# Channel attention and a gated layer, fp32 by split products: sums of squares by accumulating DMAs, high parts by ScalarE, and seven products for every pair of two more batches

## The chip, the cores and the metric

One core of a Trainium2 chip runs the whole program. The metric is the device time of one execution in microseconds. TensorE is called PE here (PEld is its weight load), VectorE DVE, ScalarE ACT, GpSimd POOL and SyncE SP.

## The reference

Four batches of q, k and v, each 6080 x 256, all float32; w_in is 256 x 2048 and w_out 2048 x 256, handed in as float64 words.

```python
qn = q / (norm(q, axis=1) + 1e-6)            # over the 6080 tokens
kn = k / (norm(k, axis=1) + 1e-6)
a  = softmax(kn.T @ qn / tau)                # 256 x 256 in each batch
x  = v @ a                                   # 24320 tokens x 256 in all
h  = x @ w_in                                # 24320 x 2048
g  = h / (1 + exp(-1.702 * h))
out = g @ w_out                              # 24320 x 256
```

## The kernel before

**Arithmetic.** A float32 product is made from parts: a high part (the value cast to fp32r) and a low part (what is left), and three matmuls, high by high, high by low and low by high (`three`, L780 in the traces). A high part is made by ACT (`cast`, L285) or, for q and k of batches 2 and 3, by a casting DMA from POOL's queue (`load_cast`, L282); a low part is a subtraction on DVE (`low`, L308). Other additions on DVE are `tt` (L293) and `minus` (L299).

**The main loop.** `a` and `w_in` are folded together for each batch, so the main loop makes `v @ (a @ w_in)`, the gate, and the product with `w_out`. A batch is cut into 6 chunks of tokens, five of 1024 and one of 960, and the 2048 hidden columns into 8 pairs of blocks. There are 4 x 6 x 8 = 192 pairs, in the order batch, chunk, pair. A pair is a product of 2 x 2 blocks, made in a Strassen-Winograd form with seven products. `front` makes the seven products before the gate into the banks X, Y and Z, with copies on ACT (ps_Y<-ps_X and others) between them, and the gate on ACT into `ga`. `back` makes the product with `w_out`, in one of two forms:

- with seven products (`is_s`): sums of blocks on DVE into `gp` (p13 of two blocks, p2, p4), their high and low parts in `gr` and `gj`, and three blocks of `ga` split into `gi`. Five products follow at once, two (`k6`, `k5`, from `gr`) at the end of the group;
- with eight: no sums, two blocks in `gi` and two in `gj`, eight products.

Pairs stand in groups, given by `groups_of`: `TWO = ((3, 1), (3, 1))` is two groups of three seven-product pairs and one eight-product pair; `THREE = ((3, 0), (3, 0), (2, 0))` has seven-product pairs alone. One bank, K, is shared within a group and is evacuated at its end three times (a, b, c), and once more (d) where the group has an eight-product pair: in the first group by ACT copies, later by additions on DVE. `groups_of` gives batch 0 (after its first chunk, which has eight products throughout) to batch 2 `TWO`, and batch 3 `THREE`.

**Preparation.** Beside the main loop of one batch the next ones are prepared. `Attention.unit` takes two tiles of 128 tokens of q and k at a time, 25 units a batch: raw tiles are loaded by SP into two buffers in turn (`ra0`, `ra1`); the scores k.T @ q go to PE (ps_s); ACT squares the raw tiles in place, and the squares are added into `acc` for the norms. For batches 2 and 3 the scores use parts: `hl` is one buffer with high and low. Batches 0 and 1 use the raw float32 values (`direct`). Batch 2's units are placed beside pairs 19 to 60, batch 3's beside 74 to 118; three pieces of softmax (`finish`) and eight `weights` follow each.

**The order.** `Plan` holds every operation with its engine, cost, lag, dependences, buffers and a due time. It places them by a list schedule forwards and backwards and emits each engine's instructions, the DMA issues of SP and POOL among them, in that fixed order. Weights come from HBM for each pair: `w` (two buffers), `wo` (three) and, for seven-product pairs, `wb`.

Of the kernel before, what the change touches and what calls it, by code (L numbers as in the profile page):

```python
# [11 lines left out]
F32 = mybir.dt.float32  # L12
# [3 lines left out]
ALU = mybir.AluOpType  # L16
# [4 lines left out]
P = 128  # L21
# [4 lines left out]
HW = CH // 2  # L26
# [162 lines left out]
FIRST = ((0, 4), (0, 4))  # L189


def groups_of(b, c):

    if b == c == 0:
        return FIRST
    return (TWO, TWO, TWO, THREE)[b]


NV = 8
# [8 lines left out]
def channel_attention_then_glu(  # L208
# [10 lines left out]
    nc = tc.nc  # L219
# [3 lines left out]
    NPAIR = DFF // (2 * P)  # L223
# [57 lines left out]
    def load_cast(dst, src, kb, deps=(), uses=(), due=0.0):  # L281
        return g.add("POOL", 800, lambda: nc.gpsimd.dma_start(dst(), src()), deps, uses, due, lag=8000)  # L282
# [12 lines left out]
    def minus(dst, a, b, n, deps, uses, due):  # L295

        return g.add(
            "DVE", dve(n),
            lambda: nc.vector.scalar_tensor_tensor(  # L299
                dst(), in0=a(), scalar=-1.0, in1=b(), op0=ALU.mult, op1=ALU.subtract,  # L300
            ),
            deps, uses, due,
        )

    def low(dst, src, hi, n, deps, uses, due):
# [132 lines left out]
    class Attention:  # L438
# [39 lines left out]
        def unit(self, u, due, after=()):  # L478
            t0, nt, pp = self.units[u]
            if t0 not in self.raw:  # L480
                t = sbuf(f"ra{u % 2}", [P, 2, UT, C], F32, "raw")
                view = (lambda i: t()[:, i, :nt, :]) if pp == P else (lambda i: t()[:pp, i, 0, :])
                ns = [
                    load(
                        lambda i=i: view(i), lambda i=i: self.rows(i, t0, nt, pp), 128 * nt, after, [t], due - 10, 7000,
                    )
                    for i in range(2)
                ]
                for o in range(nt):
                    self.raw[t0 + o] = (t, o, ns)  # L490
            buf, o, _ = self.raw[t0]
            ready = [n for j in range(nt) for n in self.raw[t0 + j][2]]
            w = 2 * nt * C
            src = lambda: buf()[:pp, :, o : o + nt, :]
            acc = self.acc
            if self.direct:
                ok, uses = ready, [buf]
            else:
                hl = sbuf("hl", [P, 2, UT, 2, C], F32R, "hl")
                hs = [  # L500
                    load_cast(
                        lambda i=i: hl()[:, i, :nt, 0, :] if pp == P else hl()[:pp, i, 0, 0, :],
                        lambda i=i: self.rows(i, t0, nt, pp), 128 * nt, after, [hl], due - 9,
                    )
                    for i in range(2)
                ]
                l = low(
                    lambda: hl()[:pp, :, :nt, 1, :], src, lambda: hl()[:pp, :, :nt, 0, :], w,
                    hs + ready, [buf, hl], due,
                )  # L510
                ok, uses = [l], [hl]
            S = self.S if self.direct else bank("Z", "s")
            news = []
            for j in range(nt):
                first = j == 0 and (u == 0 or not self.direct)

                def fn(j=j, first=first):
                    for i in range(NC2):
                        ci = slice(i * P, (i + 1) * P)
                        out = S()[:, i * C : (i + 1) * C]  # L520
                        begin = first and i == 0
                        if self.direct:
                            nc.tensor.matmul(  # L523
                                out, lhsT=buf()[:pp, 1, o + j, ci], rhs=buf()[:pp, 0, o + j, :],
                                start=begin, stop=True, skip_group_check=True,
                            )
                            continue
                        for m, (l, r) in enumerate(((0, 0), (0, 1), (1, 0))):
                            nc.tensor.matmul(  # L529
                                out, lhsT=hl()[:pp, 1, j, l, ci], rhs=hl()[:pp, 0, j, r, :],  # L530
                                start=begin and m == 0, stop=True, skip_group_check=True,
                            )

                n = g.add(
                    "PE", 864 if self.direct else 720, fn, ok + [self.first] + news[:1], [*uses, S], due + 2 + 0.1 * j,
                )
                if first and self.direct:
                    self.first = n
                news.append(n)
            if u == 0:  # L540
                self.acc_n = [g.add(
                    "ACT", act(w), lambda: nc.scalar.activation(acc(), src(), AF.Square), ok, [buf, acc], due + 0.5,
                )]
            else:

                sq = buf if self.b else sbuf(f"w{u % 2}", [P, 2, UT, C], F32, "sq")
                sqv = (lambda: src()) if self.b else (lambda: sq()[:pp, :, :nt, :])
                if self.b == 1:
                    ok = news
                s = g.add(  # L550
                    "ACT", act(w),
                    lambda: nc.scalar.activation(sqv(), src(), AF.Square), ok, [buf, sq], due + 1,
                )
                a = lambda: acc()[:pp, :, :nt, :]
                self.acc_n = [tt(
                    a, a, sqv, ALU.add, w, [s, *self.acc_n], [sq, acc], due + 1.5,
                )]
            if self.direct:
                self.last += news
            else:  # L560
                total = self.S
                self.last = [
                    g.add("DVE", dve(HW), lambda: nc.vector.tensor_copy(total(), S()), news, [S, total], due + 2.5)
                    if u == 0 else
                    tt(
                        lambda: total(), lambda: S(), lambda: total(), ALU.add, HW, news + self.last, [S, total],
                        due + 2.5,
                    )
                ]
# [150 lines left out]
    def values(b, c, due, after=(), eng="DVE"):  # L720
        o, w = chunks[c]
        hw = w // 2
        raw = sbuf("vr", [P, NC2, CH], F32, "v_raw")
        src = vT[b, :, o : o + w].rearrange("(c p) n -> p c n", p=P)
        r = load(lambda: raw()[:, :, :w], lambda: src, 1024, after, [raw], due - 40)
        blk = lambda j, n: (lambda: raw()[:, j, n * hw : (n + 1) * hw])
        B11, B12, B21, B22 = blk(0, 0), blk(0, 1), blk(1, 0), blk(1, 1)
        done = {}

        def split(m, x, deps, at, uses):  # L730
            t = sbuf(f"v{vslot[0] % NV}", [P, 2, HW], F32R, "v")
            vslot[0] += 1
            h = cast(lambda: t()[:, 0, :hw], x, hw, deps, [*uses, t], at)
            l = low(lambda: t()[:, 1, :hw], x, lambda: t()[:, 0, :hw], hw, [h], [*uses, t], at + 0.3)
            done[m] = (t, l)
            return l


        vt = sbuf("vt", [P, HW], F32, "v_t")
        P1 = lambda: vt()[:, :hw]  # L740
        p1 = tt(P1, B11, B12, ALU.add, hw, [r], [raw, vt], due - 20, eng)
        p3 = tt(B12, B12, B22, ALU.add, hw, [p1], [raw], due - 16, eng)
        split(M5, P1, [p1], due, [vt])
        s11 = split(M1, B11, [r, p1], due + 0.7, [raw])
        s21 = split(M2, B21, [r], due + 2, [raw])
        p2 = tt(B11, P1, B22, ALU.add, hw, [p1, s11], [raw, vt], due + 2.2, eng)
        split(M6, B11, [p2], due + 2.5, [raw])
        split(M7, B12, [p3], due + 4, [raw])
        split(M3, B22, [r, p3], due + 4.5, [raw])
        p4 = tt(B21, B21, B11, ALU.add, hw, [p2, s21], [raw], due + 3, eng)  # L750
        split(M4, B21, [p4], due + 6, [raw])
        return done
# [79 lines left out]
    def back(ck, u, fr, wo, wb, t):  # L832
# [87 lines left out]
        def evac(name, deps, at):  # L920
            prev = ck.tot.get(name)
            if prev is None:
                s = sbuf("k" + name, [P, HW], F32, "k" + name)
                n = cast(lambda: s()[:, :hw], lambda: K[0]()[:, :hw], hw, deps, [K[0], s], at, psum=True)
            else:
                s = prev[0]
                n = tt(
                    lambda: s()[:, :hw], lambda: K[0]()[:, :hw], lambda: s()[:, :hw], ALU.add, hw,
                    [*deps, prev[1]], [K[0], s], at,
                )  # L930
            ck.tot[name] = (s, n)
            return n
# [226 lines left out]
```

## Time and profile before

| | us |
|---|---|
| median of 3 runs | 2116.87 |
| lowest, highest | 2116.82, 2120.28 |
| the profiled execution, its own time | 2116.12 |
| its span in the trace | 2114.4 |
| PE, DVE, ACT busy | 2082.2, 1918.6, 1620.3 |

The span runs from the first instruction to the last. A busy time is the union of an engine's instructions; PE's matmuls overlap in its pipe, so a PE that is busy all the time need not issue at its full rate, and the distance between starts says more.

### The profile page before, as it was taken

The page shows a single profiled execution, that of the slowest core. Times are in us where ns is not written, and L with a number is a line of the kernel's source. Part 1 is how long each engine was busy: PE and PEld are TensorE (multiplying, and loading weights), DVE is VectorE, ACT ScalarE, POOL GpSimd, SP SyncE. Part 2 cuts the span into 40 slices and gives each one's busy share as a digit, 9 for nine tenths or more (in the row PEclk, how much of TensorE's full clock was granted, in tenths as well). Part 3 has the DMA queues.
Part 4 walks back from the last instruction along what each step waited for, and adds up shares of the span by engine and source line. Part 5 has one row for each costly group of instructions (what it writes and reads, how often), then busy time and mean ns, then how long its engine had stood idle before and what let it go on. Part 6 is the DMA issues. An engine that isn't in the chain of part 4 may idle for free.

```text
span 2114.4 us, 27101 instructions
## 1 busy us (share of the span) xinstructions
PE 2082.2 (98%) x9658; PEld 1737.6 (82%) x9658; DVE 1918.6 (91%) x2395; ACT 1620.3 (77%) x2361; POOL 76.7 (4%) x110
## 2 busy tenths in 40 slices
PE   9799999999999999999999999999999999999998
PEld 8688787888888888888888888888888888888887
DVE  8898898989999989889989898898988999999997
ACT  6677886877777877878767777778787778778875
POOL 0000001000000000000000000000000000000000
PEclk9899999999999999999999999999999999999999
DMA  9997787777777567877776776668756656665663
GB/s 352 333 338 263 264 291 264 255 236 250 253 254 265 192 235 260 296 263 255 244 258 214 264 266 216 212 217 290 281 189 219 226 208 212 232 231 186 245 213 130
DMA packets 210135, 521.90 MB, mean 247 GB/s; under 512 B 16464, under 2 KB 88144, under 8 KB 208976
## 3 DMA queue, kind: packets, MB, share of 16 engines
q1 hardware_dynamic: 184080, 495.25, 65.9%
q0 software_dynamic: 25920, 24.91, 5.1%
q8 instruction: 77, 1.26, 0.2%
q14 instruction: 58, 0.48, 0.1%
HBM read 453.25 MB, written 66.85 MB: 246 GB/s over the span
## 4 chain that ended last, share of the span: by engine, by line
PE 80%; DVE 9%; DMA 6%; ACT 3%; issue 1%; SPq 1%; POOL 0%; DVEq 0%; ACTq 0%
PE ps_o L780 23%; PE ps_X L780 16%; PE ps_k L780 14%; PE ps_Y L780 11%; PE ps_Z L780 10%; PE ps_s L529 3%; PE ps_w L696 2%; DMA hl<-in_k 2%; DVE gp L293 1%; PE ps_s L523 1%; DVE gi L308 1%; DMA out_T<-oc 1%; DVE ga L293 1%; DMA v_raw<-in_vT 1%; DVE acc L293 1%
## 5 line engine op out<-in xcount | busy, mean ns | idle before, releaser
L780 PE MATMUL ps_X<-v,w 128*128 128x512 f32 (+1 forms) x1728 | 485.1, 389 | 0.8 <-ACT ps_Z L285 0.7
L780 PEld LDWEIGHTS ps_X<-v,w 128*128 128x128 f32 x1728 | 321.2, 188 | 68.7 <-ACT ps_Z L285 3.1
L780 PE MATMUL ps_o<-gi,wo 128*128 128x512 f32 (+1 forms) x1404 | 375.7, 388 | 1.3 <-DVE gi L308 1.3
L806 ACT ACTIVATE ga<-ga 128x512 f32<-128x512 f32 (+1 forms) x384 | 238.4, 627 | 163.0 <-DVE ga L293 161.5
L308 DVE TENSOR_TENSOR gi<-ga,gi 128x1536 fp32r<-128x1536 f32 (+2 forms) x192 | 311.1, 1621 | 27.4 <-ACT gi L285 26.6
L780 PE MATMUL ps_Y<-v,w 128*128 128x512 f32 (+1 forms) x1152 | 325.5, 391 | 3.9 <-ACT ps_Y L285 2.5
L780 PE MATMUL ps_Z<-v,w 128*128 128x512 f32 (+1 forms) x1152 | 323.7, 389 | 1.0 <-ACT ps_Z L285 0.5
L780 PE MATMUL ps_o<-gj,wo 128*128 128x512 f32 (+1 forms) x1152 | 310.6, 389 | 1.1 <-DVE gj L308 0.7
L780 PEld LDWEIGHTS ps_o<-gi,wo 128*128 128x128 f32 x1404 | 262.7, 188 | 54.5 <-DVE gi L308 1.6
L285 ACT CAST gi<-ga 128x1536 fp32r<-128x1536 f32 (+2 forms) x192 | 264.3, 1376 | 7.7 <-PE ps_k L780 3.0
L780 PEld LDWEIGHTS ps_Z<-v,w 128*128 128x128 f32 x1152 | 215.0, 188 | 47.9 <-ACT ps_Z L285 2.5
L780 PEld LDWEIGHTS ps_o<-gj,wo 128*128 128x128 f32 x1152 | 215.2, 188 | 46.3 <-DVE gj L308 1.7
L780 PEld LDWEIGHTS ps_Y<-v,w 128*128 128x128 f32 x1152 | 212.2, 188 | 49.5 <-ACT ps_Y L285 5.9
L780 PE MATMUL ps_k<-gr,wb 128*128 128x512 f32 (+1 forms) x900 | 239.6, 388 | 0.0
L308 DVE TENSOR_TENSOR gr<-gp,gr 128x1024 fp32r<-128x1024 f32 (+1 forms) x150 | 181.0, 1207 | 23.2 <-ACT gr L285 23.2
L293 DVE TENSOR_TENSOR gp<-ga 128x1024 f32<-128x1024 f32 (+1 forms) x150 | 181.4, 1209 | 21.1 <-ACT ga L806 18.1
L780 PEld LDWEIGHTS ps_k<-gr,wb 128*128 128x128 f32 x900 | 168.3, 188 | 34.0 <-DVE kb L293 0.3
L308 DVE TENSOR_TENSOR gj<-gp,gj 128x1024 fp32r<-128x1024 f32 (+1 forms) x150 | 181.0, 1206 | 9.9 <-ACT gj L285 9.8
L285 ACT CAST gr<-gp 128x1024 fp32r<-128x1024 f32 (+1 forms) x150 | 156.2, 1042 | 43.9 <-DVE gp L293 33.4
L285 ACT CAST gj<-gp 128x1024 fp32r<-128x1024 f32 (+1 forms) x150 | 156.2, 1041 | 8.4 <-DVE gp L293 7.4
L293 DVE TENSOR_TENSOR ga<-ps_Y,m 128x512 f32<-128x512 f32 (+1 forms) x192 | 130.4, 679 | 25.9 <-PE ps_Y L780 25.4
L285 ACT COPY ps_Y<-ps_X 128x512 f32<-128x512 f32 (+1 forms) x192 | 110.7, 577 | 52.4 <-PE ps_X L780 51.2
(120 smaller groups left out, 2783.9 us busy)
## 6 DMA issues: line engine op xcount, KB each, us to landing
w<-w_d SPq DMA_DIRECT2D x184, 896.0 KB, 5.3
wo<-wout_d SPq DMA_DIRECT2D x150, 640.0 KB, 5.5
wb<-wout_d SPq DMA_DIRECT2D x150, 256.0 KB, 4.7
wo<-wout_d SPq DMA_DIRECT2D x42, 512.0 KB, 5.8
w_d<-wst SPq DMA_DIRECT2D x24, 896.0 KB, 6.1
v_raw<-in_vT SPq DMA_DIRECT2D x20, 1024.0 KB, 8.3
out_T<-oc SPq DMA_DIRECT2D x80, 256.0 KB, 5.1
wi<-win_d SPq DMA_DIRECT2D x32, 512.0 KB, 5.2
```

The lines of the kernel that those rows point to most:

```text
L285: return g.add("ACT", act(n, psum), lambda: nc.scalar.copy(dst(), src()), deps, uses, due)
L293: return g.add("DVE", dve(n), lambda: nc.vector.tensor_tensor(dst(), a(), b(), op=op), deps, uses, due)
L308: lambda: nc.vector.tensor_tensor(dst(), src(), hi().bitcast(F32), op=ALU.subtract),
L523: nc.tensor.matmul(out, lhsT=buf()[:pp, 1, o + j, ci], rhs=buf()[:pp, 0, o + j, :], start=begin, stop=True, skip_group_check=True,)
L529: nc.tensor.matmul(out, lhsT=hl()[:pp, 1, j, l, ci], rhs=hl()[:pp, 0, j, r, :], start=begin and m == 0, stop=True, skip_group_check=True,)
L696: nc.tensor.matmul(pb()[:, i * 2 * P : (i + 1) * 2 * P], lhsT=at.aT()[:, l, j, ci], rhs=wi()[:, m, j, :], start=i == 0 and n == 0, stop=Tr ...
L780: nc.tensor.matmul(dst, lhsT=l(a), rhs=r(b), start=begin and n == 0, stop=True, skip_group_check=True,)
L806: lambda: nc.scalar.activation(dst(), src(), AF.Gelu_apprx_sigmoid, scale=sign), deps, uses, at,
```

## The change

Three things change. The squares of q and k of batches 2 and 3 are still made by ACT in place, but are added into `acc` by a DMA from POOL's queue that accumulates (SBUF to SBUF, `add_dma`), not by DVE; the planner is told of a lag of 9 us. The high parts of q and k of these batches are one ACT cast from the raw tile, in place of two casting DMAs. And batches 1 and 2 get `THREE` in place of `TWO`. The switches VSUM and KSUM are off, so their branches (in `values` and in `evac`) emit nothing.

```diff
+VSUM = lambda b, c: False
+QSUM = lambda b: b >= 2
+HIACT = True
+KSUM = 0
+ALAG = 9000
...
-    return (TWO, TWO, TWO, THREE)[b]
+    return (TWO, THREE, THREE, THREE)[b]
...
+    def add_dma(dst, more, deps, uses, due):
+
+        return g.add(
+            "POOL", 1200, lambda: nc.gpsimd.dma_start(dst(), more(), accum_op=ALU.add), deps, uses, due, lag=ALAG,
+        )
...
                 hs = [
+                    cast(lambda: hl()[:pp, :, :nt, 0, :], src, w, ready, [buf, hl], due - 1)
+                ] if HIACT else [
                     load_cast(
...
-                self.acc_n = [tt(
-                    a, a, sqv, ALU.add, w, [s, *self.acc_n], [sq, acc], due + 1.5,
-                )]
+                if QSUM(self.b):
+                    self.acc_n = [add_dma(a, sqv, [s, *self.acc_n], [sq, acc], due + 1.5)]
+                else:
+                    self.acc_n = [tt(
+                        a, a, sqv, ALU.add, w, [s, *self.acc_n], [sq, acc], due + 1.5,
+                    )]
```

## Rows read from the trace of the kernel before

**Rows 1.** The page: busy times, granted clock in 40 slices, the casting DMAs' queue.
```profile
PE 2082.2 (98%) x9658; PEld 1737.6 (82%) x9658; DVE 1918.6 (91%) x2395; ACT 1620.3 (77%) x2361; POOL 76.7 (4%) x110
...
PEclk9899999999999999999999999999999999999999
...
q0 software_dynamic: 25920, 24.91, 5.1%
```

**Rows 2.** Timeline of PE alone, in batch 0: start, us, what, [idle before].
```profile
327.63 0.84 PE L780 MATMUL ps_o<-gj,wo 128*128 128x512 f32 x3
328.31 0.84 PE L780 MATMUL ps_X<-v,w 128*128 128x512 f32 x3
...
331.03 0.84 PE L780 MATMUL ps_o<-gi,wo 128*128 128x512 f32 x3
332.69 0.36 PE L529 MATMUL ps_s<-hl 128*128 128x256 f32 x1 [0.81 <-DMA hl<-in_k]
333.91 1.57 PE L529 MATMUL ps_s<-hl 128*128 128x256 f32 x11 [0.87 <-DVE hl L308]
```

**Rows 3.** Busy times by stretch: batch 0 after chunk 0, batch 1, batch 2.
```profile
core 0: us, PE busy (x) PEld busy (x) DVE busy (x) ACT busy (x) POOL busy (x), PEclk, DMA share, GB/s
...
204.10:635.50 431.40, 426.67 (x2027) 356.55 (x2027) 390.43 (x480) 332.91 (x487) 28.36 (x39) 1.00 0.76 257
635.50:1143.60 508.10, 505.19 (x2390) 423.69 (x2389) 460.90 (x565) 394.19 (x580) 30.03 (x41) 1.00 0.74 251
1143.60:1637.40 493.80, 492.22 (x2286) 410.74 (x2285) 438.13 (x540) 384.26 (x567) 16.43 (x23) 1.00 0.68 238
```

**Rows 4.** The same in batch 3: chunk 1, chunk 4, chunks 1 to 4.
```profile
1718.70:1792.10 73.40, 73.40 (x324) 60.25 (x323) 71.28 (x84) 60.66 (x90) 0.00 (x0) 1.00 0.60 216
...
1949.00:2022.30 73.30, 73.23 (x321) 59.65 (x320) 70.27 (x83) 58.62 (x87) 0.00 (x0) 1.00 0.63 225
...
1718.70:2022.30 303.60, 303.40 (x1328) 247.71 (x1327) 292.90 (x341) 246.21 (x357) 0.00 (x0) 1.00 0.62 220
```

**Rows 5.** Timeline of DVE alone, in batch 0.
```profile
313.50 1.21 DVE L293 TENSOR_TENSOR gp<-ga 128x1024 f32<-128x1024 f32 x1
314.63 1.75 DVE L308 TENSOR_TENSOR gi<-ga,gi 128x1536 fp32r<-128x1536 f32 x1
316.30 0.68 DVE L299 SCALAR_TENSOR_TENSOR oc<-ps_o,kc 128x512 f32<-128x512 f32 x1
316.90 0.68 DVE L293 TENSOR_TENSOR kd<-ps_k,kd 128x512 f32<-128x512 f32 x1
```

**Rows 6.** The stretches of rows 3, DVE's instructions on the tile acc alone.
```profile
204.10:635.50 431.40, 20.73 (x17) 1.00 0.76 257
635.50:1143.60 508.10, 22.78 (x20) 1.00 0.74 251
1143.60:1637.40 493.80, 14.23 (x13) 1.00 0.68 238
```

**Rows 7.** Busy times in the stretch with batch 2's weights (columns as rows 3).
```profile
719.50:890.60 171.10, 169.31 (x801) 141.21 (x800) 152.15 (x207) 134.23 (x201) 3.12 (x3) 1.00 0.69 250
```

**Rows 8.** The tile hl: its casting DMAs (issue, count), and landings.
```profile
L282 POOL DMA_DIRECT2D hl<-in_k x50: 527/721/736, 320.5 to 1339.8; - x50
...
DMA to landing us min/median/max: 2.1/6.0/12.0
```

**Rows 9.** The tile raw in batches 0 to 2: additions of squares (first, last start), landings.
```profile
L293 DVE TENSOR_TENSOR acc<-acc,raw x48: 675/1218/1227, 347.0 to 1353.8; 128x1024 f32<-128x1024 f32 x44, 128x512 f32<-128x512 f32 x2, 64x512 f32<-64x512 f32 x2
...
DMA to landing us min/median/max: 2.6/5.8/8.8
```

**Rows 10.** ACT's groups in batches 1 and 2: count, busy, mean ns, idle before.
```profile
L285 ACT CAST gi<-ga 128x1536 fp32r<-128x1536 f32 x60 | 89.0, 1484 | 4.6 <-PE ps_k L780 2.4 <-PE ps_o L780 1.0
L285 ACT CAST gr<-gp 128x1024 fp32r<-128x1024 f32 x60 | 63.1, 1052 | 16.0 <-DVE gp L293 13.1 <-PE ps_k L780 2.7
```

**Rows 11.** The chain that ended last, in order of time: start, us, what.
```profile
320.52 9.52 DMA hl<-in_k
330.04 2.59 issue
...
349.51 8.72 DMA hl<-in_k
...
1173.45 8.57 DMA hl<-in_k
```

## What was predicted

> **What bounds the kernel now.** I read the page first: PE is busy 98% of the span and its granted clock, the PEclk line, is full but for the first slices [rows 1]. That matmul busy time counts a matmul's wait in the pipe too, so I went on to the pace: in a timeline of PE alone three matmuls of 512 columns start every 0.68 us, 0.2267 us each, and this hardly changes for whole stretches [rows 2]. Then the busy times by stretch [rows 3]: batch 0 after its first chunk, batch 1, batch 2. The reader is to see two things. PE is busy almost throughout, and DVE has 9.5%, 9.3% and 11.3% left. So PE sets the time, through the number of its matmuls, and DVE is the second engine close behind. Batch 3 shows what the seven-product form alone looks like, since it has it already: over four chunks without any preparation of scores or weights, PE issued 1328 matmuls in 303.6 us, 0.2286 us each, 0.8% over its pace, while DVE was busy 96.5%; in the first of these chunks DVE was busy 97.1% [rows 4]. That is the fullest DVE that the trace shows, and PE hardly suffered from it.
>
> **PE: the term that gains.** A pair without the seven products makes 8 products of 3 matmuls behind the gate (24), one with them 7 (21). Batches 1 and 2 have 6 chunks each with two such pairs: 24 pairs, 72 matmuls fewer. Sixty have 512 columns, 60 x 0.2267 = 13.6 us; the twelve of the two short chunks have 480, by share 0.2126 us each, 2.6 us. Together 16.2 us. PE sets the pace there, so all of it counts unless another engine takes over. Batches 1 and 2 took 508.1 + 493.8 = 1001.9 us; PE alone would make that 985.7.
>
> **DVE: the term that takes some back.** What one more DVE instruction costs is read from the distance between starts, as consecutive ones overlap by 0.08 us: 1.13 us for 1024 elements, 1.67 for 1536, 0.60 for 512 [rows 5]. Such a pair gains the two-block sum (1.13), two single sums (2 x 0.60), the low part of gr (1.13), and its gi is of three blocks instead of two (1.67 - 1.13 = 0.54); the low part of gj was there before, in another form. That is 4.0 us. A chunk also evacuates K nine times instead of eight, six of them by additions on DVE instead of four: 2 x 0.60. So 2 x 4.0 + 1.2 = 9.2 us a chunk, 8.7 at 480 columns, 10 x 9.2 + 2 x 8.7 = 109.4 us in all.
>
> Against it the additions of the squares go. In these two batches they are 19 and 12 (20 and 13 rows less the one addition of each softmax) [rows 6]: 22.78 + 14.23 less 2 x 0.68 and less an overlap of 0.086 each make 33.0 us. DVE was busy 460.90 + 438.13 = 899.0 us [rows 3]; it will be 899.0 + 109.4 - 33.0 = 975.4. In 985.7 us that is 99.0%, above anything that the trace shows. In the stretch with the weights of batch 2 it is worse: 152.15 us of 171.1 [rows 7] become 152.2 + 18.4 - 1.1 = 169.5, in 168.4 us of PE. There DVE must hold PE up.
>
> What two engines that are both nearly full lose to each other no row shows. Bounds: if DVE can be filled no further than the 97.1% of rows 4, the two batches take 975.4 / 0.971 = 1004.5 us, 2.6 more than now; if it can be filled wholly, 985.7, 16.2 less. At 97.1% PE lost almost nothing, so the limit lies above it; but as the weights' stretch does not fit, I take 98.0%, nearer the row: 995.3 us, 6.6 less than now.
>
> By a rule of the Trainium skill ("VectorE: DVE Perf Modes", section "The DRAIN you can't avoid") a DVE instruction waits until the pipe of the one before is empty, and chaining doesn't avoid it; the same section allows an earlier start where nothing holds the instruction. Taken strictly it would add the 0.086 us to each instruction and make this change a loss (the last rival below). The trace does not agree: the start at 314.63 us lies before the end of the instruction at 313.50, which took 1.21 [rows 5].
>
> **The squares by DMA.** Forty-eight additions leave DVE (17 of them in batch 0, where PE is the bound and their 19 us are worth nothing by themselves) and become DMAs from POOL's queue. POOL has nothing else to do then; its 100 casting DMAs go. The accumulate moves 512 KB and also reads its target. Nearest rows: the casting DMAs, 256 KB at most, land in 6.0 us in the median and 12.0 at most [rows 8], the raw loads of the same units in 2.6 to 8.8 us [rows 9]. I bound it by 2 and 18 us (one and a half times the longest), and take 9. What waits for it: the next accumulate, behind it in POOL's queue, and the raw buffer, which the load two units later needs. A unit comes every 17.0 us ((635.5 - 347.0) / 17) [rows 6, 9], so each of two buffers has 34 us; load, cast, low part and square take 5.8 + 1.05 + 1.13 + 1.06 = 9.0 us, which leaves 25 us with the waits in between. So no cost up to about 20 us. Beyond that the raw load blocks SP's queue, with the w, wo and wb loads behind it.
>
> **The high parts by ScalarE.** Fifty casts of 1024 elements at 1.05 us [rows 10] come onto ACT, 31 or so in these two batches (33 us). The 24 pairs add one cast of gr (1.05) and widen gi (1.48 - 1.05), 35 us, less 12 evacuations of 0.58. ACT goes from 394.19 + 384.26 = 778 to about 840 us in 990, 85% [rows 3]; in rows 4 it ran at 82.6% (60.66 of 73.40) without harm. Cost nothing, hidden beside PE; if that cover went, it would show as ps_Y and ps_Z evacuations late. In return the low part no longer waits for a casting DMA, whose landings are in the chain: the first of batch 0 took 9.52 us and 2.59 more until its waiter started [rows 11], and PE stood from 331.71 (331.03 and three starts of 0.2267) to 332.69, and again, after one matmul of 0.12, to 333.91 [rows 2]: 2.1 us. Of the three other long ones in the chain [rows 11] I count nothing, which leaves up to 2 us unclaimed. So 2.1 us less, between 0 and 4.
>
> The added wb loads (24 of 256 KB) and wider wo are 9 MB, less than the 24.91 MB of q and k that the casting queue read a second time [rows 1]; DMA share is 0.74 or below in both batches [rows 3]. Nothing. Head, batch 0's other chunks, batch 3 and the tail are as before: nothing, give or take a few us by which the replanned order shifts.
>
> **Sum.** 2116.1 us of the profiled execution (span 2114.4 and 1.7 around it) - 6.6 - 2.1 = 2107.4. The median of the runs shown, 2116.87, lies 0.8 higher, which makes 2108; with the bounds of DVE's limit leaning to the better side, as PE lost nothing at 97.1%, I give 2107.
>
> **Rivals.**
> PE keeps its pace in full, DVE follows at 99%: 2116.1 - 16.2 - 2.1 = 2098, up to 2 less if the small stalls shrink. For it: rows 4, where DVE is at 97.1% and PE undisturbed. Against: the weights' stretches, which don't fit.
> DVE takes back everything: at 97.1 to 97.4% the two batches come out at 1001.4 to 1004.5 us, total 2113 to 2117: no change. The point that decides is 975.4 / 1001.9 = 97.4%.
> Slower, one mechanism: DVE becomes the bound in batches 1 and 2 and needs more idle time than 2.6%. Place: the group ends and the weights' stretches, where a gi low part waits for its cast on ACT while nothing else is ready. At 95.9%, the share of the chunk at 1949.0 [rows 4], 975.4 / 0.959 = 1017.1 us, 15.2 more: 2129. Against it: in that chunk PE set the pace, so DVE's idle time there is what PE left.
> The accumulates are late: over 20 us each, the raw loads hold up SP's queue. At 25 us it is 5 us on some 48 units, of which I take half as hidden by w's second buffer: about 120 us slower, 2230. Against it: none of the casting DMAs took over 12.0 us [rows 8].
> DVE instructions that don't overlap: 565 + 540 [rows 3] + 120 - 31 = 1194 instructions of 0.086 us, up to 103 us: 1078 us for the two batches, 2192.
>
> **Chances.** The forecast (2102 to 2112) 0.47; PE in full 0.25; no change 0.15; DVE the bound 0.09; late accumulates 0.03; no overlap 0.01. What a measurement here tells from no change is about 0.2%, 4.2 us: faster is below 2112.6, and the first two cases make 0.72; same 0.16, with a little of the forecast's edge; slower 0.12. The range takes in the PE-bound case and the no-change case to a little way into the slower one: 2096 to 2122.
>
> **What would show it.** PE's matmuls should be 9586 (9658 - 72); DVE busy over batches 1 and 2 near 975 us and its idle time in them 1 to 3%; no low part of hl waiting for a DMA; 48 accumulates, landing under 20 us, with no SP wait on them of note. More PE waits on DVE (ga, gi, gp, gr) in batches 1 and 2 are expected, most of them about the weights. Wrong would be: the batches not shorter though DVE idles over 3%, which would mean latency along one chain, not load; a stretch in which w or wo arrive late behind a raw load; or batch 3 changed.

## The result, and the profile after

The changed kernel takes 2099.72 us in the median of 4 runs (2096.14 to 2101.60), the kernel before on the same chip 2118.57 us (2116.82 to 2121.57): ratio 0.9911, 95% interval 0.9899 to 0.9923, or 18.9 us. The forecast was 2107 (2096 to 2122). The profiled execution of the changed kernel took 2096.14 us, its fastest, and its span is 20.1 us shorter than that of before. The profiled execution of before lies 2.5 us under the median of its runs here, that of the change 3.6, so differences of spans lean some 1.2 us to the better side, and stretches of the change alone some 3 us.

From the page of the kernel after, the lines that answer to [rows 1]; instructions have other line numbers now (L780 became L815, L285 L292, L293 L300, L308 L321, L523 L538, L593 L611):

```profile
PE 2063.3 (99%) x9586; PEld 1723.9 (82%) x9586; DVE 1966.3 (94%) x2467; ACT 1691.6 (81%) x2423; POOL 49.7 (2%) x58
...
PEclk9999999999999999999999999999999999999999
...
q0 software_dynamic: 7168, 23.86, 6.4%
```

PE has the 72 matmuls less that were counted, at the same full granted clock. Busy times by stretch of the kernel after: up to the first pair of batch 1, batch 1, batch 2, both batches, the rest. And of the kernel before, the first stretch and both batches in one (columns as in [rows 3]):

```profile
0.00:625.90 625.90, 610.30 (x2902) 513.08 (x2903) 549.41 (x749) 488.38 (x695) 18.40 (x26) 0.99 0.84 281
625.90:1133.40 507.50, 502.91 (x2378) 421.36 (x2377) 492.24 (x609) 425.66 (x608) 17.38 (x19) 1.00 0.77 259
1133.40:1617.60 484.20, 482.25 (x2246) 403.44 (x2245) 473.38 (x587) 404.57 (x585) 13.89 (x13) 1.00 0.74 252
625.90:1617.60 991.70, 985.15 (x4622) 824.81 (x4621) 965.62 (x1195) 830.23 (x1191) 31.27 (x32) 1.00 0.75 256
1617.60:2094.30 476.70, 467.86 (x2066) 385.99 (x2064) 451.29 (x525) 372.95 (x540) 0.00 (x0) 1.00 0.60 211
```

```profile
0.00:635.50 635.50, 615.63 (x2916) 516.48 (x2917) 570.69 (x770) 470.53 (x676) 30.19 (x46) 0.99 0.81 279
635.50:1637.40 1001.90, 997.41 (x4674) 834.43 (x4673) 899.03 (x1104) 778.45 (x1146) 46.46 (x64) 1.00 0.71 244
```

The first stretch lost 9.6 us, both batches 10.2, the rest 0.3 (477.0 to 476.7). Work slips over the cuts: of the 72 matmuls 14 are missing in the first stretch, 52 in the two batches, 6 in the rest. The 14 are products of batch 0's own last chunk (480 columns) that stand behind the cut now; at 0.2126 us they are 3.0 us, so 6.6 us of the first stretch came from something else. The 52 are 11.8 us at 0.2267, of which 1.6 were lost. PE's waits in the two batches of the kernel after, all of them (us, times, longest):

```profile
PE ps_Z L815 <- DMA w<-w_d: 5.2, 5, 2.5
PE ps_t L683 <- ACT ga L841: 0.9, 1, 0.9
PE ps_k L815 <- DVE gi L321: 0.4, 1, 0.4
```

So its matmuls waited for late loads of w (0.5 us before) and hardly for DVE. DVE is at 97.0% in batch 1 and 97.8% in batch 2. A single chunk of batch 2 shows that it goes further:

```profile
1465.60:1545.10 79.50, 79.50 (x363) 66.15 (x362) 79.21 (x100) 66.15 (x98) 0.00 (x0) 1.00 0.72 256
```

DVE is busy 79.21 of 79.50 us there, 99.6%, while PE issues 363 matmuls in them, 0.2190 us each, no slower than in [rows 2] (there are short ones among them). The timeline of DVE alone, of the kernel after, in that chunk:

```profile
1489.42 1.76 DVE L321 TENSOR_TENSOR gi<-ga,gi 128x1536 fp32r<-128x1536 f32 x1
1491.09 1.23 DVE L300 TENSOR_TENSOR gp<-ga 128x1024 f32<-128x1024 f32 x1
1492.22 0.69 DVE L306 SCALAR_TENSOR_TENSOR oc<-ps_o,kc 128x512 f32<-128x512 f32 x1
1492.83 0.69 DVE L300 TENSOR_TENSOR ga<-ps_Y,m 128x512 f32<-128x512 f32 x1
```

Each instruction starts about 0.09 us before the one ahead of it ends, as in [rows 5]. The rule of the Trainium skill that the prediction weighed ("VectorE: DVE Perf Modes", section "The DRAIN you can't avoid"), taken strictly, would have given 2192 us; this trace does not bear that out.

The tiles hl and acc of the kernel after: the high parts' casts, the accumulates and their landings, and of SP's waits the one on an accumulate (us, times, longest):

```profile
L292 ACT CAST hl<-raw x50: 609/1051/1066, 325.9 to 1326.4; 128x1024 fp32r<-128x1024 f32 x46, 128x512 fp32r<-128x512 f32 x2, 64x512 fp32r<-64x512 f32 x2
```

```profile
L315 POOL DMA_DIRECT2D acc<-raw x48: 847/856/1214, 338.7 to 1336.1; - x48
...
DMA to landing us min/median/max: 3.6/6.1/11.2
```

```profile
SPq L285 <- DMA acc<-raw: 4.8, 3, 3.5
```

The accumulates land in 6.1 us in the median, and the raw loads wait 4.8 us for them in the whole run.

What changed in the first stretch is seen at its head, in the timeline of PE alone: first before, then after.

```profile
65.63 1.84 PE L593 MATMUL ps_n<-ones,acc 128*128 128x1 f32 x8 [8.80 <-DVE acc L293]
```

```profile
57.66 0.95 PE L611 MATMUL ps_n<-ones,acc 128*128 128x1 f32 x8
60.41 2.08 PE L538 MATMUL ps_s<-raw 128*128 128x256 f32 x4 [1.79 <-DMA raw<-in_k]
```

Before, PE stood 8.80 us until DVE had added the squares of batch 0. After, that wait is gone, though no operation of the head was changed. The wait also cost clock. From 59.6 to 73.3 us, before and after:

```profile
59.60:73.30 13.70, 7.67 (x22) 6.53 (x23) 12.45 (x27) 4.51 (x7) 1.13 (x1) 0.50 0.91 303
59.60:73.30 13.70, 12.89 (x54) 11.19 (x55) 11.77 (x27) 7.79 (x12) 1.03 (x1) 0.88 1.03 367
```

Before, the granted clock stood at 0.50, the lower level (1.2 GHz), after PE had come to a stand, and PE issued 22 matmuls; after, it was 0.88 in the mean, and PE issued 54. What changed in the head is the emitted order: DVE's first 149 instructions stand in another order than before (found from the two programs' lists of instructions).

### The profile page after: what moved, and what is told of

The parts are those of the page before. It is cut to its first block, busy times and chain, and to the rows that moved or that the text cites. A ratio compares the mean times of both kernels' runs of the same rounds, so it can differ in the third digit from the quotient of the medians.

```text
span 2094.3 us, 27083 instructions
## 1 busy us (share of the span) xinstructions
PE 2063.3 (99%) x9586; PEld 1723.9 (82%) x9586; DVE 1966.3 (94%) x2467; ACT 1691.6 (81%) x2423; POOL 49.7 (2%) x58
## 3 DMA queue, kind: packets, MB, share of 16 engines
q0 software_dynamic: 7168, 23.86, 6.4%
## 4 chain that ended last, share of the span: by engine, by line
PE 77%; DVE 10%; DMA 7%; issue 3%; ACT 3%; POOLq 0%; SPq 0%; POOL 0%; DVEq 0%; ACTq 0%
PE ps_o L815 21%; PE ps_X L815 15%; PE ps_k L815 15%; PE ps_Z L815 10%; PE ps_Y L815 10%; DMA w<-w_d 3%; PE ps_s L544 3%; DVE gp L300 2%; PE ps_w L714 2%; DVE gi L321 1%; DVE acc L300 1%; PE ps_s L538 1%; DVE ga L300 1%; DMA w_d<-wst 1%; DMA out_T<-oc 1%
## 5 line engine op out<-in xcount | busy, mean ns | idle before, releaser
L815 PE MATMUL ps_X<-v,w 128*128 128x512 f32 (+1 forms) x1728 | 484.6, 389 | 1.6 <-ACT ps_Z L292 1.5
L815 PEld LDWEIGHTS ps_X<-v,w 128*128 128x128 f32 x1728 | 321.8, 188 | 68.6 <-ACT ps_Z L292 3.8
L815 PE MATMUL ps_o<-gi,wo 128*128 128x512 f32 (+1 forms) x1260 | 340.2, 388 | 1.5 <-DVE gi L321 1.5
L321 DVE TENSOR_TENSOR gi<-ga,gi 128x1536 fp32r<-128x1536 f32 (+2 forms) x192 | 324.4, 1690 | 12.9 <-ACT gi L292 12.4
L815 PE MATMUL ps_Z<-v,w 128*128 128x512 f32 (+1 forms) x1152 | 324.3, 390 | 7.5 <-DMA w<-w_d 7.3
L815 PE MATMUL ps_Y<-v,w 128*128 128x512 f32 (+1 forms) x1152 | 324.2, 390 | 0.4 <-ACT ps_Y L292 0.4
L815 PE MATMUL ps_o<-gj,wo 128*128 128x512 f32 (+1 forms) x1152 | 315.1, 388 | 1.1 <-DVE gj L321 0.7
L292 ACT CAST gi<-ga 128x1536 fp32r<-128x1536 f32 (+2 forms) x192 | 274.7, 1431 | 5.2 <-PE ps_k L815 1.9
L815 PEld LDWEIGHTS ps_o<-gi,wo 128*128 128x128 f32 x1260 | 235.4, 188 | 49.4 <-DVE gi L321 2.7
L815 PE MATMUL ps_k<-gr,wb 128*128 128x512 f32 (+1 forms) x1044 | 273.6, 388 | 0.0
L815 PEld LDWEIGHTS ps_Z<-v,w 128*128 128x128 f32 x1152 | 214.9, 188 | 55.6 <-DVE gr L321 2.9
L815 PEld LDWEIGHTS ps_o<-gj,wo 128*128 128x128 f32 x1152 | 215.4, 188 | 45.4 <-DVE gj L321 1.1
L815 PEld LDWEIGHTS ps_Y<-v,w 128*128 128x128 f32 x1152 | 212.7, 188 | 44.4 <-ACT ps_Y L292 3.4
L300 DVE TENSOR_TENSOR gp<-ga 128x1024 f32<-128x1024 f32 (+1 forms) x174 | 210.9, 1212 | 19.6 <-ACT ga L841 16.5
L815 PEld LDWEIGHTS ps_k<-gr,wb 128*128 128x128 f32 x1044 | 195.0, 188 | 38.8 <-DVE kb L300 0.3
L321 DVE TENSOR_TENSOR gr<-gp,gr 128x1024 fp32r<-128x1024 f32 (+1 forms) x174 | 210.8, 1211 | 10.6 <-ACT gr L292 10.5
L321 DVE TENSOR_TENSOR gj<-gp,gj 128x1024 fp32r<-128x1024 f32 (+1 forms) x174 | 210.7, 1211 | 6.5 <-ACT gj L292 6.4
L292 ACT CAST gr<-gp 128x1024 fp32r<-128x1024 f32 (+1 forms) x174 | 181.1, 1041 | 36.7 <-DVE gp L300 27.9
L292 ACT CAST gj<-gp 128x1024 fp32r<-128x1024 f32 (+1 forms) x174 | 181.0, 1040 | 11.9 <-DVE gp L300 10.3
L292 ACT COPY ps_Y<-ps_X 128x512 f32<-128x512 f32 (+1 forms) x192 | 110.4, 575 | 56.0 <-PE ps_X L815 54.7
L815 PE MATMUL ps_k<-gi,wo 128*128 128x512 f32 (+1 forms) x522 | 146.5, 389 | 1.1 <-DMA wo<-wout_d 0.7
```

The source lines that it names most:

```text
L292: return g.add("ACT", act(n, psum), lambda: nc.scalar.copy(dst(), src()), deps, uses, due)
L300: return g.add("DVE", dve(n), lambda: nc.vector.tensor_tensor(dst(), a(), b(), op=op), deps, uses, due)
L321: lambda: nc.vector.tensor_tensor(dst(), src(), hi().bitcast(F32), op=ALU.subtract),
L815: nc.tensor.matmul(dst, lhsT=l(a), rhs=r(b), start=begin and n == 0, stop=True, skip_group_check=True,)
```

## The experiments

The theory after the result: PE's 72 matmuls are worth nearly their 16.2 us because DVE can be filled to about 99% and no further, and the rest comes from batch 0 and above all its head, where the list schedule came out better once the casting DMAs were gone. The rivals: the gain is the casting DMAs' own cost all along batches 0 to 2; the head's gain is the place of the sum of v, or any new order; the seven products would gain without DVE's relief.

All kernels are the changed one with switches set otherwise, except where it says "before". Times are medians; "less" is the difference to the median of the kernel before on the same chip, measured beside it.

| kernel | seven products | squares by DMA | high parts by ACT | us | less | ratio (95%) |
|---|---|---|---|---|---|---|
| the change | yes | yes | yes | 2099.72 | 18.9 | 0.9911 (0.9899-0.9923) |
| groups_only | yes | no | no | 2114.12 | 2.4 | 0.9982 (0.9970-0.9994) |
| no_groups | no | yes | yes | 2108.14 | 8.4 | 0.9957 (0.9942-0.9971) |
| high_only | no | no | yes | 2107.17 | 9.4 | 0.9955 (0.9940-0.9970) |
| groups_high | yes | no | yes | 2107.44 | 10.3 | 0.9958 (0.9943-0.9973) |
| groups_sums | yes | yes | no | 2122.80 | -5.0 | 1.0020 (1.0004-1.0037) |

**The parts alone and in pairs.** The seven products without the rest:

```diff
-QSUM = lambda b: b >= 2
-HIACT = True
+QSUM = lambda b: False
+HIACT = False
```

> Seven products for every pair in batches 1 and 2, but the squares' sums stay on DVE and the high parts on the casting DMAs. If DVE's relief is what lets PE's 16.2 us through: DVE would need 899.0 + 109.4 = 1008 us in these two batches, more than the 1001.9 us they took before, so they take 1010 to 1020 us, DVE idle under 1% in them, and the whole is 8 to 18 us slower than before (2126 to 2137). If the planner can hide DVE's work anyway: 2100 to 2104. In both the head stays at its 99.6 us before the first pair, since DVE's order there is that of before.

The rest without the seven products:

```diff
-    return (TWO, THREE, THREE, THREE)[b]
+    return (TWO, TWO, TWO, THREE)[b]
```

> The sums by DMA and the high parts by ScalarE, batches 1 and 2 as before (eight products in two pairs of a chunk). By the forecast: 2 us less, where a casting DMA came late in batch 0, and nothing for DVE's relief, 2115 to 2117. By the rival, that some 7 us of the gain come from the head, where this kernel has the order of the changed one (the sum of batch 0's squares ahead of v's blocks on DVE): 2107 to 2111, the head at 92 to 94 us instead of 99.6.

ScalarE's high parts alone (the edit of no_groups, and QSUM as in groups_only):

> High parts by ScalarE alone. The head has the order of the changed kernel here too. By the rival: head 92 to 94 us, 2107 to 2111. By the forecast: 2115 to 2117, the first late casting DMA of batch 0 (2.1 us) gone and nothing else.

The change without the accumulating DMAs (QSUM as in groups_only):

> Seven products and the high parts by ScalarE, the sums kept on DVE. By the theory that DVE can be filled to 98 or 99% and no further: batches 1 and 2 take 1001 to 1008 us, as with the groups alone (1004.6), DVE idle under 1.5% in them, and batch 1 starts 6 to 10 us earlier than before: 2106 to 2114. If the casting DMAs were what made the groups alone slow: 990 to 995 us, 2097 to 2103.

The seven products alone bring little (2.4 us), though they take the same 72 matmuls away. Both cases of their expectation missed: DVE's 1008 us came out as 992.66 busy, and the head did not stay as before. DVE stands in a third order there, PE's norms start without a wait, and the first stretch is 6.2 us shorter with 6 matmuls fewer:

```profile
55.07 0.95 PE L611 MATMUL ps_n<-ones,acc 128*128 128x1 f32 x8
```

```profile
0.00:629.30 629.30, 611.98 (x2910) 514.65 (x2911) 568.27 (x769) 470.67 (x676) 35.34 (x46) 0.99 0.81 282
```

So the 2.4 us are those of another order in batch 0; the two batches took 2.8 us more than before. Both batches in groups_only, then in groups_high:

```profile
629.30:1634.00 1004.70, 990.35 (x4615) 821.35 (x4614) 992.66 (x1224) 809.19 (x1159) 47.59 (x64) 1.00 0.73 253
```

```profile
627.30:1630.90 1003.60, 993.51 (x4628) 823.58 (x4628) 992.87 (x1226) 832.03 (x1192) 4.56 (x2) 1.00 0.67 239
```

Two kernels that differ in their high parts have the same DVE time and the same length: 98.8% and 98.9%. PE's share is 98.6% and 99.0% there, down from 99.6% before. This is DVE's limit. Beside ScalarE's high parts, the seven products alone add nothing measurable (2107.44 against 2107.17), the accumulates alone nothing (2108.14), both together some 8 us (2099.72). The accumulates are worth something only where the seven products fill DVE, as the prediction had it; ScalarE's high parts are worth 9.4 us by themselves, which it did not have; they lie in the first stretch (626.6 us in high_only), while its two batches took 1001.7 us, as before.

The change with the casting DMAs back (HIACT as in groups_only):

> Seven products and the sums by DMA, the casting DMAs kept. If DVE's relief is what batches 1 and 2 need and the high parts pay in the head and batch 0 alone: batches 1 and 2 take 988 to 995 us, as in the changed kernel (991.7), and batch 1 starts near 635 us as before, since DVE's order in the head is not that of the changed kernel: 2103 to 2110. If the high parts on ScalarE are also needed for the dense stretches: 995 to 1003 us there, 2108 to 2117.

This expectation missed: it is slower than before. In the stretch from 883 to 1300 us, batch 3's scores, its busy times, then those of the change:

```profile
883.00:1300.00 417.00, 404.58 (x1882) 335.97 (x1881) 393.80 (x464) 322.73 (x458) 50.17 (x64) 0.99 0.89 279
```

```profile
883.00:1300.00 417.00, 412.67 (x1950) 347.00 (x1949) 406.79 (x479) 353.32 (x498) 18.85 (x22) 1.00 0.80 261
```

The DMA engines are busy 89% of it, not 80%, and PE issues 68 matmuls fewer in the same time, 15.4 us at its pace. PE's waits there on w (us, times, longest) in groups_sums, two of its DMA issues with their KB and landing, and its timeline of POOL, where casting DMAs stand behind an accumulate that waits for ACT's squares:

```profile
PE ps_Z L815 <- DMA w<-w_d: 6.2, 5, 3.1
PE ps_X L815 <- DMA w<-w_d: 3.0, 1, 3.0
```

```profile
w<-w_d SPq DMA_DIRECT2D x39, 896.0 KB, 7.0
hl<-in_k POOLq DMA_DIRECT2D x22, 256.0 KB, 9.2
```

```profile
983.60 0.91 POOL L315 DMA_DIRECT2D acc<-raw  x1 [15.58 <-ACT raw L567]
984.19 1.06 POOL L289 DMA_DIRECT2D hl<-in_q  x1
984.89 1.09 POOL L289 DMA_DIRECT2D hl<-in_k  x1
```

The change, in that stretch:

```profile
PE ps_Z L815 <- DMA w<-w_d: 4.3, 3, 2.5
```

```profile
w<-w_d SPq DMA_DIRECT2D x40, 896.0 KB, 5.9
```

PE waited 4.9 us more for w than in the change, and 3.2 us for other things (1.1 of them for hl). Twice, about waits of 1.86 and 3.08 us, the granted clock stood at 0.50, the lower level, for 3.4 us; at half the pace the two cost at most 3.4 us together. That is 11.5 of the 15.4 us; the profiled execution (2118.1) is one of the faster ones. That the two sorts of DMA crowd each other, on POOL's queue and on the engines, is argued from these rows; how much each of these costs was not separated.

**DVE's limit by dose.** One of the additions of a pair is made twice, in 48 pairs of batches 1 and 2, 48 x 0.60 = 28.8 us.

```diff
+            if u % 2 == 0 and ck.b in (1, 2):
+                p2 = tt(lambda: gp()[:, 1, :hw], lambda: gp()[:, 0, :hw], blk(3), ALU.add, hw, [p2], [ga, gp], t + 9.5)
```

> The changed kernel with 48 additions of 512 elements made twice on DVE (p2, in every other pair of batches 1 and 2): 28.8 us more for DVE, which idles 26 us in them. If DVE has become the second bound there, 10 to 29 us slower than the changed kernel: 2110 to 2129. If PE alone sets the time: 2098 to 2102.

The same in a kernel with all three parts of the change undone:

> The same 48 additions made twice in the kernel before, where DVE idles 103 us in batches 1 and 2: 0 to 3 us slower, 2117 to 2120, by both theories. A longer time would mean that the added wait in the chain of the block sums costs, and not DVE's load.

On the change it gave 2113.66 us (ratio 0.9980, 0.9971 to 0.9991), 13.9 more than without it (14.8 with each taken against the kernel before beside it); on the kernel before 2116.27 (0.9996, 0.9987 to 1.0005), no difference. Both batches, in the change with the additions (its profiled execution is the slowest of ten):

```profile
630.80:1638.50 1007.70, 997.01 (x4634) 827.67 (x4633) 992.36 (x1245) 833.43 (x1196) 30.55 (x32) 1.00 0.76 253
```

Again 98.5%. Three programs stop at 98.5 to 98.9% over these batches, the change stays below at 965.62 / 991.70 = 97.4%, PE's pace setting the time.

**Where ScalarE's high parts gain.** With neither the seven products nor the accumulates, first with ACT's cast for one unit only, the first of batch 2, then for those of batch 3 only:

```diff
-                ] if HIACT else [
+                ] if self.b == 2 and u == 0 else [
```

> The kernel before, but one unit of 50, the first of batch 2, gets its high parts from ScalarE instead of two casting DMAs. DVE's first 149 instructions then stand in the order that they have in the changed kernel, and not in that of before. If the gain of the high parts (9 us) comes from how the head is ordered: batch 1 starts 6 to 9 us earlier (635.5 before) and the whole takes 2107 to 2111. If it is gathered at the late casting DMAs, unit by unit: 2.1 us for this unit's, 2114 to 2116.

```diff
-                ] if HIACT else [
+                ] if self.b == 3 else [
```

> The kernel before with the high parts of batch 3 alone by ScalarE, 25 units, not one of them in batch 0. DVE's first 149 instructions stand as in the kernel before. If the gain of the high parts is the head and the first unit: 0 to 2 us, 2115 to 2118, batch 1 starting within 3 us of 635.5. If each late casting DMA costs: 3 to 6 us faster.

The one unit of 50 gave 2108.03 us (0.9957, 0.9941 to 0.9974), 9.6 less than before, as much as all of them. The 25 units of batch 3 gave 2114.87 (0.9989, 0.9980 to 0.9998), 2.9 less, a little more than expected; in its trace the first stretch is 2.4 us shorter, though the first of these casts starts at 904.3 us. So beside the first unit the other 49 units' casting DMAs cost nothing that shows. The timeline of PE's norms in high_first and in high_b3:

```profile
58.06 0.95 PE L611 MATMUL ps_n<-ones,acc 128*128 128x1 f32 x8
```

```profile
65.04 1.83 PE L611 MATMUL ps_n<-ones,acc 128*128 128x1 f32 x8 [8.17 <-DVE acc L300]
```

And batch 0 in high_first, cut ahead of the place where the first casting DMA was late, and behind it, then the whole stretch; the kernel before below it:

```profile
0.00:288.70 288.70, 276.28 (x1305) 232.76 (x1306) 255.29 (x402) 212.27 (x301) 2.74 (x8) 0.98 0.86 309
288.70:376.30 87.60, 87.11 (x417) 72.95 (x416) 78.42 (x94) 69.05 (x101) 5.90 (x8) 1.00 0.83 281
0.00:627.90 627.90, 614.99 (x2916) 517.90 (x2917) 569.17 (x770) 473.06 (x677) 28.67 (x44) 0.99 0.81 281
```

```profile
289.30:382.60 93.30, 90.87 (x430) 75.32 (x430) 80.63 (x98) 69.41 (x101) 7.33 (x10) 1.00 0.79 269
```

By the whole stretch (2916 matmuls in both) it is 7.6 us shorter. Ahead of 289 us it is 0.6 us shorter and holds 13 matmuls more (2.9 us): 3.5. In the cut with the late landing it is 5.7 shorter with 13 matmuls fewer: 2.8. The last 1.3 lie behind. So removing one unit's two casting DMAs does two things: the stall of [rows 2] goes, and the planner, which places everything at once, emits another order for the head. DVE's first 149 instructions stand in one and the same order in the change, high_first, high_only, no_groups, groups_high, alag6 (below) and more_dve_after, and in that of before in high_b3 and more_dve_before.

The 3.5 us are of one execution each. Chunk 1's first matmul on ps_X, with 897 matmuls ahead of it in all ten traces, starts at 198.5 to 202.0 us in the seven kernels with the new order (high_first is the last of them) and at 202.8 to 205.6 in the three with the old (before is the last). So the orders differ by 4.3 us in the mean, and executions with one order by up to 3.5. In PE's waits up to 205 us the 8.8 for the norms are gone, and those for raw tiles have grown; before, then high_first:

```profile
PE ps_s L523 <- DMA raw<-in_k: 4.5, 3, 3.0
PE ps_s L538 <- DMA raw<-in_k: 8.5, 4, 3.8
```

With the small ones this is 4.2 us less. The clock does not explain it alone: between 20 and 205 us it stood at the lower level for 13.7 us before and for 10.2 in high_first, which is worth at most half of the 3.5 us between them.

Is it the sum of the norms going ahead of the additions on v? In the kernel before, v's first due time is moved:

```diff
-    V[0, 0] = values(0, 0, -100.0, at.raw[T][2] if TAIL else at.raw[T - 1][2])
+    V[0, 0] = values(0, 0, -70.0, at.raw[T][2] if TAIL else at.raw[T - 1][2])
```

> The kernel before with one due time changed: v's blocks of the first chunk due at -70 instead of -100, so that DVE sums batch 0's squares ahead of them. If the head's order is what shortens it, the first pair comes 4 to 8 us earlier and the whole takes 2110 to 2115; if the shorter head is chance of one execution, 2117 to 2120. Batches 1 and 2 stay within 3 us of before.

PE's wait at the norms is gone there too (they start at 56.95 us), yet the time is 2116.22 (0.9999, 0.9990 to 1.0009), between the two that were expected. In its profiled execution, the slowest of ten, the first stretch is 635.2 us long, with short new waits in and about the first chunk (2.2 us in two, 1.3, 1.1 in two). So the one visible wait is not the explanation by itself; which part of the head's order carries the gain stays open.

**How much hangs on the order.** The change with the accumulates' lag planned as 6 us, near what they took:

```diff
-ALAG = 9000
+ALAG = 6000
```

> The changed kernel with 6 us instead of 9 told to the planner as the accumulating DMA's lag (it landed in 6.1 us in the median): the same work in another order. It shows how far a replanned order alone moves the time: within 4 us of the changed kernel, 2096 to 2104, if the gain does not hang on one lucky order; more than that would say that it does.

2101.11 us (0.9930, 0.9906 to 0.9955): as the change, within the spread of its runs, with DVE's head in the same order. Both batches, in its profiled execution (2102.62 us):

```profile
628.00:1626.00 998.00, 988.72 (x4628) 825.08 (x4627) 969.08 (x1198) 832.61 (x1193) 30.68 (x32) 1.00 0.76 255
```

The same work took 6.3 us more than the 991.7 of the change, which come from its fastest execution, and DVE was not full, at 97.1%.

**One step further.** Seven products from batch 0's second chunk on:

```diff
-    return (TWO, THREE, THREE, THREE)[b]
+    return (THREE, THREE, THREE, THREE)[b]
```

> The changed kernel with seven products for every pair of batch 0 too, after its first chunk: 30 matmuls fewer, 6.7 us of PE, and about 46 us more on DVE, which idles 67 us in batch 0. By the theory that DVE may be filled to 97 to 99% without loss: 5 to 7 us faster than the changed kernel, 2093 to 2095. If every replanned order may lose in the head what it gains elsewhere: 2095 to 2103.

2095.53 us (0.9893, 0.9879 to 0.9908): the best version, 22.1 us less than before and some 3 to 4 less than the change, a little less of a gain than the 5 to 7 that were expected.

## Why the prediction was right, and where not

- **PE is the bound, 72 matmuls, 16.2 us.** Right: 9586 matmuls. Without the seven products the time was 2108.1, with them 2099.7: they brought 8.4 us, or 10.4 with each taken against the kernel before beside it. So 6 to 8 of the 16.2 were taken back, where 9.6 had been predicted. (By the profiled executions they brought 13.7, but that is the slowest run of no_groups against the fastest of the change.)
- **DVE takes some back.** The right mechanism wherever DVE has more to do than in the change, shown by the dose (nothing before, 13.9 us after) and by groups_only. For the change itself its two sizes were off. The load was 975.4 us by the sum and 965.6 in the trace, with 1195 instructions against 1194: where DVE is nearly full, instructions that had stood alone start before the one ahead of them ends, so their busy times overlap (1070 of 1194 in the two batches, 884 of 1103 before). The limit was taken as 98.0% and is 98.5 to 98.9%. With the measured pair, 965.6 / 0.985 = 980.3 us, DVE no longer sets the end of the two batches and PE does, at 985.7, or 990.1 with the 52 matmuls that fell into them; the trace has 991.7. The waits on DVE that were expected did not come (0.4 us). What took back 6 to 8 us in the executions about the median no trace shows; that it was DVE is not shown.
- **The squares by DMA.** Right in the main: 6.1 us to landing where 9 was taken, 4.8 us of SP's waits, and what they take off DVE (33 us by the sum, 27.3 between groups_high and the change) is what lets PE's saving through. But a sign that the prediction had named came: PE waited 5.2 us for late w in the two batches, against 0.2 in groups_high, without accumulates, and 1.2 in no_groups, without the seven products. It was not the blocked queue of the prediction, as SP waited 1.3 us for accumulates there; what made w late was not tested.
- **The high parts by ScalarE.** The step that failed: "2.1 us less, between 0 and 4", and the head "nothing, give or take a few us". They measured 9.4 us alone. By the cuts of high_first, the one with the late first landing, the term that was seen, gave 2.8 of it. Of the rest, 3.5 lie ahead of it, where no casting DMA ran before and only the planner's order differs, and 1.3 behind it in batch 0; these the prediction had left out as a few us of either sign. ACT, at 83.7% of the two batches, did no harm, as said.
- **DMA engines "nothing".** Right for the change, but for the late w, and for a reason that was not seen: accumulates beside the casting DMAs cost some 7 us net (5.0 slower than before, where the seven products alone were 2.4 faster), so ScalarE's high parts also make room for the accumulates.
- **The rivals.** The total lies outside the 2102 to 2112 of the forecast's own case and came near "PE keeps its pace in full" (2098), but by luck, as a sum of other terms: the median holds 6 to 8 us that were taken back and some 7 more from the high parts than were counted. "DVE takes back everything" is what the two batches of groups_only show. None of the late accumulates, of DVE as a loss, or of instructions that don't overlap was seen.

## What to carry to other kernels

Two engines at 98% and 91% are two limits: cut the work of the first together with work of the second, and judge the two cuts as a pair (beside ScalarE's high parts each alone added nothing here, both together 8 us). Where one planner orders the whole program, taking away a single operation can reorder a place far from it; compare the emitted orders before a gain is put down to the operation itself. Here the accumulates paid only once the casting DMAs had left the same queue and engines.

## What was not expected of the hardware

DVE was filled to 99.6% over 79.5 us beside PE at its pace and ACT at 83%, and to 98.8% over a millisecond in groups_only, where it held PE up. An accumulating DMA of 512 KB from SBUF to SBUF occupies POOL 0.86 us and lands in 6.1 us (3.6 to 11.2); 48 of them took 6.4% of the DMA engines' span, more than the 5.1% of the 100 casting DMAs, though they are 23.86 MB against 24.91.
